# First attention of a fused attention and mixture kernel: where the sums of exponentials are formed, the order of the keys' products, the first weight decoding and the dummy products

## The chip, the cores and the metric

The kernel runs on one core of one Trainium2 chip. The metric is the device time of one execution in microseconds (us). Three executions before the change gave 999.26, 996.85 and 998.99, median 998.99. The core has five engines with a queue each, worked off in order: PE (matrix products; PEld is its loading of weights), DVE (vector), ACT (scalar functions), POOL (general), SP (here only issues DMA transfers). They wait for each other by semaphores.

## The reference

For 8 batches of 8 heads with 576 positions of 64 dimensions, a memory attention with 32 slots, then two layers of experts:

```python
a = np.exp(phi - np.max(phi, axis=2, keepdims=True))       # over the 576 positions
a = a / (np.sum(a, axis=2, keepdims=True) + 1e-09)
k_m = np.einsum('bhsm,bhsd->bhmd', a, k);  v_m = np.einsum('bhsm,bhsd->bhmd', a, v)
scores = (1 / np.sqrt(64)) * np.matmul(q, k_m.transpose(0, 1, 3, 2))
attn = softmax(scores);  out = np.matmul(attn, v_m)
# x: 4608 x 512
h = max(x @ w1, x @ w2, x @ w3);  y = h @ w_out             # weights arrive as float64
# second layer: of 8 experts the one with the largest gate, gate_w * relu(y @ w1[e]) @ w2[e]
```

## The kernel before, in words

Batches go one after another. The attention of batch b + 1 is woven into the first expert layer of batch b by a table of due times; the attention of batch 0 stands at the program's start, written out by hand (lines 843 to 893), and a scheduler turns that into one instruction order for each engine.

`phi` of a batch lies as 128 partitions by (4 pairs of heads j, 9 chunks c, 32 slots). A partition half `par` (64 partitions) belongs to one head of a pair. `at_max`, `at_col` and `at_sub` (lines 223 to 248) subtract the maximum, `at_exp` (L252) takes the exponential in two halves, pairs 0 and 1 first, then 2 and 3. `at_asum` (L254, through `over_chunks`, L218 to L221) adds the nine chunks elementwise: on DVE, for batch 1 on POOL. `at_km` (L260) multiplies: for each chunk, pair and half one product of 64 rows by 32 columns with 128 moving columns (64 of k, 64 of v), 72 products (L268), accumulated over chunks; each is two records in the trace, since its operands are float32. Then two products with a column of ones (L277) add the 64 partitions of `asum`. `rs` (L287, L288) is the reciprocal; with it ACT scales keys and values (`kx`, `vx`, L294 and L299). `at_kvT` transposes them on PE, ACT copies the result (`kT`, `vT`), DVE transposes q (`at_qT`, L319), PE forms the scores (L332), DVE transposes them back (L340), subtracts the maximum (L348), and so on to `at_hi` and `at_lo`, the first operand of the expert layer (`m1_step`, L101 to L103, with the maximum of the three branches on DVE, L458).

The float64 weights of the first layer come in 24 parts of 512 KB through six raw buffers. `w_done(n)` decodes one part to float32: ACT reads one word of each number (L151), DVE does four passes (L154, L161, L164, L167). A raw buffer is free after the last pass, and SP then issues the load of the part six further on. `after` (L125) is a copy of one element on ACT; it only makes what follows wait for its source.

`keep` (L840) issues products into a scratch bank that nobody reads. They hold TensorE busy. `WARM` (17 products, L758) is the same ahead of the first transpose.

Loads of batch 0 are issued by SP in the order of the code: phi, weights part 0, k, v, weights part 1, four of q, weights parts 2 to 5.

## Time and profile before

| | before |
|---|---|
| three executions | 999.26, 996.85, 998.99 us (median 998.99) |
| profiled execution | 1001.34 us, span of its instructions 999.6 us |
| PE busy | 970.2 us of the span (97%) |
| DVE busy | 563.5 us (56%) |
| ACT busy | 374.3 us (37%) |
| POOL busy | 150.8 us (15%) |
| granted TensorE clock, mean | 0.989 |

The busy time of PE counts the dummy products too, and it is an average over a start, a middle and an end with different limits. A time of a row is counted from the start of the span.

### The profile page before, as it was taken

The numbers are of one execution on the slowest core, as the hardware profiler recorded it, in microseconds if no ns is written. First come the engines' busy times: TensorE is split into PE (matmuls) and PEld (weight loads), VectorE is DVE, ScalarE is ACT, GpSimd is POOL, SyncE is SP. The second block draws the span as 40 slices with busy tenths as digits, with TensorE's granted clock in tenths as the row PEclk, the third lists the DMA queues.
The fourth block names the chain that finished last, engine by engine and source line by source line (L and its number), as shares of the span: only waits on it lengthen the run. The fifth ranks groups of instructions, "written<-read, shape, count | busy, mean of one in ns | idle before, by whom it ended". The sixth has DMA issues, their size and how long they took to land. (4 is left out here: it accounts for less than half of the span.)

```text
span 999.6 us, 20600 instructions
## 1 busy us (share of the span) xinstructions
PE 970.2 (97%) x8326; PEld 854.5 (85%) x8326; DVE 563.5 (56%) x1285; ACT 374.3 (37%) x816; POOL 150.8 (15%) x263
## 2 busy tenths in 40 slices
PE   7987999999999999999999999999999999999996
PEld 5566888889899888988889989898989898989985
DVE  5999768474674737747275626261717171726331
ACT  2574443433444334334356324150506060604220
POOL 0001021110211202122021030302021212111020
PEclk8998999999999999999999999999999999999998
DMA  9394342132221323010137426271717161625210
GB/s 330 114 338 152 120 125 92 48 121 96 101 80 38 129 86 121 13 37 2 48 104 244 134 58 207 44 220 35 229 32 231 33 206 52 204 57 159 96 34 26
DMA packets 59107, 114.79 MB, mean 115 GB/s; under 512 B 7687, under 2 KB 20999, under 8 KB 59008
## 3 DMA queue, kind: packets, MB, share of 16 engines
q1 hardware_dynamic: 48480, 94.01, 28.6%
q0 software_dynamic: 4768, 9.94, 4.3%
q10 hardware_dynamic: 5760, 9.48, 2.5%
q8 instruction: 67, 1.10, 0.5%
q14 instruction: 32, 0.26, 0.1%
HBM read 94.00 MB, written 19.44 MB: 113 GB/s over the span
## 5 line engine op out<-in xcount | busy, mean ns | idle before, releaser
L101 PE MATMUL ps_m<-at_hi,u_hi 128*128 128x288 f32 x576 | 175.4, 305 | 2.7 <-DVE hx L458 2.5
L103 PE MATMUL ps_m<-at_hi,u_lo 128*128 128x288 f32 x576 | 170.6, 297 | 0.2 <-ACT u_lo L435 0.2
L102 PE MATMUL ps_m<-at_lo,u_hi 128*128 128x288 f32 x576 | 169.9, 295 | 0.0
L101 PE MATMUL ps_x<-yh,w1h 128*128 128x288 f32 (+1 forms) x544 | 160.9, 296 | 0.3 <-DVE xh L625 0.3
L103 PE MATMUL ps_x<-yh,w1l 128*128 128x288 f32 (+1 forms) x544 | 159.9, 294 | 0.0
L102 PE MATMUL ps_x<-yl,w1h 128*128 128x288 f32 (+1 forms) x544 | 159.9, 294 | 0.0
L101 PEld LDWEIGHTS ps_m<-at_hi,u_hi 128*128 128x128 f32 x576 | 108.3, 188 | 25.2 <-issue 12.4
L458 DVE TENSOR_TENSOR hx<-hx,ps_m 128x288 f32<-128x288 f32 x192 | 86.1, 448 | 75.1 <-PE ps_m L103 67.5
L98 POOL TENSOR_TENSOR h_lo<-hx,h_hi 128x288 fp32r<-128x288 f32 x84 | 70.5, 839 | 380.9 <-ACT h_hi L97 359.6
L654 POOL DMA_DIRECT2D out_dram<-o x144 | 70.8, 498 | 352.6 <-DVE o L651 313.0
L101 PE MATMUL ps_m<-h_hi,wo_hi 128*128 128x288 f32 x384 | 115.0, 299 | 5.3 <-DVE hx L458 3.4
L102 PE MATMUL ps_m<-h_lo,wo_hi 128*128 128x288 f32 x384 | 113.7, 296 | 0.0
L103 PE MATMUL ps_m<-h_hi,wo_lo 128*128 128x288 f32 x384 | 113.6, 296 | 0.0
L103 PEld LDWEIGHTS ps_m<-at_hi,u_lo 128*128 128x128 f32 x576 | 108.0, 188 | 4.0 <-issue 3.1
L651 DVE TENSOR_SCALAR o<-ps_x,scal 128x512 f32<-128x512 f32 x32 | 24.0, 751 | 154.8 <-PE ps_x L103 154.8
L102 PEld LDWEIGHTS ps_m<-at_lo,u_hi 128*128 128x128 f32 x576 | 108.4, 188 | 0.9 <-issue 0.6
L101 PE MATMUL ps_x<-w2h,xh 128*128 128x512 f32 x272 | 107.6, 396 | 0.0
L102 PE MATMUL ps_x<-w2l,xh 128*128 128x512 f32 x272 | 107.5, 395 | 0.0
L103 PE MATMUL ps_x<-w2h,xh 128*128 128x512 f32 x272 | 107.4, 395 | 0.0
L101 PEld LDWEIGHTS ps_x<-yh,w1h 128*128 128x128 f32 x544 | 102.1, 188 | 1.8 <-ACT xh L622 0.5
L102 PEld LDWEIGHTS ps_x<-yl,w1h 128*128 128x128 f32 x544 | 102.1, 188 | 0.4
L103 PEld LDWEIGHTS ps_x<-yh,w1l 128*128 128x128 f32 x544 | 102.1, 188 | 0.0
(210 smaller groups left out, 1592.8 us busy)
## 6 DMA issues: line engine op xcount, KB each, us to landing
raw<-in_moe_w_dram SPq DMA_DIRECT2D x72, 512.0 KB, 4.8
raw<-y_dram SPq DMA_DIRECT2D x36, 288.0 KB, 3.1
w<-in_moe_w_dram SPq DMA_DIRECT2D x18, 512.0 KB, 5.2
kv_t<-in_k_dram SPq DMA_DIRECT2D x8, 1152.0 KB, 6.8
kv_t<-in_v_dram SPq DMA_DIRECT2D x8, 1152.0 KB, 9.7
q_t<-in_q_dram SPq DMA_DIRECT2D x32, 288.0 KB, 3.3
y_dram<-y_sb ACTq DMA_DIRECT2D x32, 288.0 KB, 2.1
out_dram<-o POOLq DMA_DIRECT2D x144, 64.0 KB, 1.9
```

Source lines behind the costliest of these rows:

```text
L98: eng.tensor_tensor(out=dst_lo, in0=src, in1=dst_hi, op=ALU.subtract)
L101: nc.tensor.matmul(out=ps, lhsT=hi_l, rhs=hi_r, start=first, stop=False)
L102: nc.tensor.matmul(out=ps, lhsT=hi_l, rhs=lo_r, start=False, stop=False)
L103: nc.tensor.matmul(out=ps, lhsT=lo_l, rhs=hi_r, start=False, stop=last)
L458: nc.vector.tensor_tensor(out=hx[0], in0=hx[0], in1=ps, op=ALU.max)
L651: nc.vector.tensor_scalar(out=o, in0=ps, scalar1=scal[:, b, t:t + 1], scalar2=None, op0=ALU.mult)
L654: nc.gpsimd.dma_start(out=out5[b, half, c], in_=o[i:i + TB])
```

## The change

In batches 0 and 1 the sums of exponentials are no longer added by DVE or POOL. PE forms them: for each chunk, pair and half one more product of the same exponentials with a column of ones, 72 products of one column, accumulated over the chunks. From batch 2 on nothing changes.

In batch 0 the keys' products run over pairs 0 and 1 for all chunks and then over pairs 2 and 3.

The decoding of weights part 0 starts behind `mb` instead of behind the exponential. The load of part 1 is issued behind the four of q. The decoding of part 1 stands behind the transposes of q. The transposes of q wait for `rs` instead of `kx`.

Dummies: 13 instead of 17 at the start; 8 and 8 with `mb` around the keys' products instead of 12 ahead; none between the products of the scores instead of 2; 1 instead of 2 behind part 2.

```diff
-    WARM = 17
+    WARM = 13
 ...
     def at_asum(b):
+        if b < 2:
+            return
 ...
-        over_chunks(asum, t, ALU.add, nc.gpsimd if b == 1 else nc.vector)
+        over_chunks(asum, t, ALU.add)
 ...
+        for js in ((0, 1), (2, 3)) if b == 0 else (range(J),):
+            for c in range(NCH):
+                for j in js:
 ...
+        if b < 2:
+            for c in range(NCH):
+                for j in range(J):
+                    for par in range(2):
+                        r0 = HP * par
+                        nc.tensor.matmul(
+                            out=pss[par][32 * j:32 * j + 32, 2 * D:2 * D + 1], lhsT=t[r0:r0 + HP, j, c, :], rhs=ones[r0:r0 + HP, 0:1],
+                            start=(c == 0), stop=(c == NCH - 1),
+                        )
 ...
-        w_load(1)
         for j in range(J):
             load_q(0, j)
-        for n in range(2, NRAW):
+        for n in range(1, NRAW):
             w_load(n)
 ...
+        w_done(0, mb[0:1, 0:1])
         at_sub(0)
-        keep(mb, 12)
+        keep(mb, 8)
         at_exp(0, 0)
-        w_done(0, inp["phi", 0][0:1, 0, 0, 0:1])
         at_exp(0, 1)
-        at_asum(0)
         at_km(0)
+        keep(mb, 8)
 ...
-        after(st["qT", 0][:, :, 0, 0, 0], kx[0:1, 0, 0, 0:J])
-        w_done(1, kx[0:1, 0, 0, 0:1])
+        after(st["qT", 0][:, :, 0, 0, 0], st["rs", 0][0:1].to_broadcast([1, J]))
         at_kvT(0)
-        turned = st["vT", 0][0:1, 0:1]
         for j in range(J):
             at_qT(0, j)
-        keep(st["qT", 0][:, 1].rearrange("p c e d -> p (c e d)")[:, :512], 2)
+        w_done(1, kx[0:1, 0, 0, 0:1])
+        turned = st["vT", 0][0:1, 0:1]
         at_scores(0)
         w_done(2, turned)
-        keep(wdst[2], 2)
+        keep(wdst[2], 1)
```

Behind line 250 a line number of the changed kernel is larger, by up to 16. PE's queue from the program's start, before (`warm` is the dummies' bank, `mb` the maxima spread out, `ps_kv` the keys' and values' bank, `w_97` the decoded weights):

```order
L758 MATMUL warm<-ones,ident 128x128 x17
L233 MATMUL ps_mx<-ident,mx 128x128
L244 MATMUL ps_mb<-ident,mb 128x128
L840 MATMUL warm<-mb,ident 128x128 x12
L268 MATMUL ps_kv<-kv_t,phi_t 32x128 x72
L277 MATMUL ps_kv<-ones,asum 128x1 x2
L305 MATMUL ps_kvT<-ident,kx 128x128 x2
L306 MATMUL ps_kvT<-ident,vx 128x128
L332 MATMUL ps_sc<-qT,kT 32x288
L840 MATMUL warm<-qT,ident 128x512 x2
L332 MATMUL ps_sc<-qT,kT 32x288 x31
L840 MATMUL warm<-w_97,ident 128x512 x2
```

The same place of PE's queue in the changed kernel:

```order
L774 MATMUL warm<-ones,ident 128x128 x13
L233 MATMUL ps_mx<-ident,mx 128x128
L244 MATMUL ps_mb<-ident,mb 128x128
L856 MATMUL warm<-mb,ident 128x128 x10
L272 MATMUL ps_kv<-kv_t,phi_t 32x128 x72
L285 MATMUL ps_kv<-ones,phi_t 32x1 x72
L856 MATMUL warm<-mb,ident 128x128 x6
L321 MATMUL ps_kvT<-ident,kx 128x128 x2
L322 MATMUL ps_kvT<-ident,vx 128x128
L348 MATMUL ps_sc<-qT,kT 32x288 x32
L856 MATMUL warm<-w_97,ident 128x512
```

Seventy-two one-column products stand between the keys' products and the transposes, and the second group of dummies is split, two of it ahead of the keys' products and six behind the sums. DVE's queue from the subtraction of the maximum to the transposes of q, before (`hc` and `asum` are the elementwise sums, `w_135` the raw part 0):

```order
L245 TENSOR_TENSOR phi_t<-phi_t,ps_mb 128x1152
L218 TENSOR_TENSOR hc<-phi_t 128x512
L219 TENSOR_TENSOR hc<-hc 128x4x64
L154 TENSOR_SCALAR w_97<-w_97 128x512
L220 TENSOR_TENSOR asum<-hc,phi_t 128x128
L161 TENSOR_SCALAR w_97<-w_97 128x512
L221 TENSOR_TENSOR asum<-asum,hc 128x128
L164 SCALAR_TENSOR_TENSOR w_97<-w_135,w_97 128x512
L167 SCALAR_TENSOR_TENSOR w_97<-w_135,w_97 128x512
L287 TENSOR_SCALAR rs<-ps_kv 128x1 x2
L288 RECIPROCAL rs<-rs 128x1 x2
L319 STREAM_TRANSPOSE qT<-q_t 128x576 x2
```

The same place of DVE's queue in the changed kernel, up to the first transpose of the scores (`w_131`, `w_144` are the raw parts 0 and 1):

```order
L245 TENSOR_TENSOR phi_t<-phi_t,ps_mb 128x1152
L154 TENSOR_SCALAR w_97<-w_97 128x512
L161 TENSOR_SCALAR w_97<-w_97 128x512
L164 SCALAR_TENSOR_TENSOR w_97<-w_131,w_97 128x512
L167 SCALAR_TENSOR_TENSOR w_97<-w_131,w_97 128x512
L302 TENSOR_SCALAR rs<-ps_kv 128x1 x2
L303 RECIPROCAL rs<-rs 128x1 x2
L335 STREAM_TRANSPOSE qT<-q_t 128x576 x4
L154 TENSOR_SCALAR w_97<-w_97 128x512 x2
L161 TENSOR_SCALAR w_97<-w_97 128x512 x2
L164 SCALAR_TENSOR_TENSOR w_97<-w_144,w_97 128x512
L356 STREAM_TRANSPOSE sc<-ps_sc 128x288
```

Four additions are gone, part 0 is decoded ahead of them all, and nothing stands between part 0 and `rs`, which waits for PE. On POOL four additions of batch 1 are gone; the rest of its queue is as before. From some 70 instructions on, the orders of DVE are the same, and PE's too but for the 72 sums of batch 1 where two products stood.

## Rows read from the trace of the kernel before

**Rows 1.** Busy time by stretch: us, PE, PEld, DVE, ACT, POOL busy (instructions), PEclk, DMA share, GB/s.

```profile
20.00:22.00 2.00, 2.00 (x3) 0.67 (x2) 2.00 (x4) 0.00 (x0) 0.00 (x0) 0.50 1.15 308
...
70.00:80.00 10.00, 7.03 (x80) 5.41 (x80) 9.86 (x18) 3.73 (x8) 3.53 (x4) 0.95 0.78 289
...
90.00:100.00 10.00, 6.64 (x36) 6.09 (x37) 10.00 (x25) 4.51 (x10) 0.00 (x0) 0.83 0.62 233
...
160.00:200.00 40.00, 40.00 (x349) 36.58 (x348) 22.68 (x52) 16.32 (x39) 5.85 (x7) 1.00 0.19 60
```

**Rows 2.** Timeline of PE, 75 to 110: start, us, instruction, idle before and releaser.

```profile
77.98 0.40 PE L101 MATMUL ps_m<-at_hi,u_hi 128*128 128x288 f32 x1 [1.70 <-DVE hx L458]
...
88.61 0.39 PE L277 MATMUL ps_kv<-ones,asum 64*128 64x1 f32 x4
88.93 0.40 PE L101 MATMUL ps_m<-at_hi,u_hi 128*128 128x288 f32 x1
...
93.53 0.40 PE L101 MATMUL ps_m<-h_hi,wo_hi 128*128 128x288 f32 x1 [2.59 <-DVE hx L458]
...
109.82 0.40 PE L101 MATMUL ps_m<-h_hi,wo_hi 128*128 128x288 f32 x1 [1.90 <-ACT y_sb L475]
```

**Rows 3.** Timeline of DVE, 70 to 85, the decoding passes beside POOL's additions.

```profile
70.87 0.42 DVE L154 TENSOR_SCALAR w<-w 128x512 f32<-128x512 f32 x1
...
74.31 1.52 DVE L154 TENSOR_SCALAR w<-w 128x512 f32<-128x512 f32 x1
75.75 1.21 DVE L167 SCALAR_TENSOR_TENSOR w<-w,w 128x512 uint32<-128x512 uint32 x1
76.89 0.67 DVE L161 TENSOR_SCALAR w<-w 128x512 uint32<-128x512 uint32 x1
...
78.82 0.68 DVE L167 SCALAR_TENSOR_TENSOR w<-w,w 128x512 uint32<-128x512 uint32 x1
...
83.09 0.42 DVE L161 TENSOR_SCALAR wod<-wod 128x512 uint32<-128x512 uint32 x1
84.67 0.69 DVE L98 TENSOR_TENSOR wo_lo<-wod,wo_hi 128x512 fp32r<-128x512 f32 x1 [1.16 <-ACT wo_hi L97]
```

**Rows 4.** Timeline of POOL, 60 to 130: first and last of four additions.

```profile
74.10 1.44 POOL L218 TENSOR_TENSOR hc<-phi_t 128x512 f32<-128x512 f32 x1 [72.78 <-ACT phi_t L252]
...
77.35 0.52 POOL L221 TENSOR_TENSOR asum<-asum,hc 128x128 f32<-128x128 f32 x1
```

**Rows 5.** Timeline of all engines, 0 to 45.

```profile
1.38 6.88 PE L758 MATMUL warm<-ones,ident 128*128 128x128 f32 x34 [1.38 <-POOL ident masks.py:199]
...
9.26 2.84 PE L840 MATMUL warm<-mb,ident 128*128 128x128 f32 x24
...
10.85 1.26 ACT L252 ACTIVATE phi_t<-phi_t 128x576 f32<-128x576 f32 x2 [1.81 <-DVE phi_t L245]
...
12.04 2.31 PE L268 MATMUL ps_kv<-kv_t,phi_t 64*32 64x128 f32 x144
...
15.61 0.22 DVE L287 TENSOR_SCALAR rs<-ps_kv 128x1 f32<-128x1 f32 x2
...
16.94 0.44 PE L305 MATMUL ps_kvT<-ident,kx 128*128 128x128 f32 x2 [2.13 <-ACT kx L294]
...
17.19 1.44 DVE L319 STREAM_TRANSPOSE qT<-q_t 128x576 f32<-128x576 f32 x2 [1.16 <-ACT qT L125]
...
23.07 0.28 PEld L332 LDWEIGHTS ps_sc<-qT,kT 32*32 32x32 f32 x32 [1.50 <-issue]
...
25.03 1.21 DVE L340 STREAM_TRANSPOSE sc<-ps_sc 128x288 f32<-128x288 f32 x3 [1.84 <-PE ps_sc L332]
...
28.41 1.42 DVE L348 TENSOR_TENSOR sc<-sc,smx 128x576 f32<-128x576 f32 x2
...
39.91 0.69 PE L101 MATMUL ps_m<-at_hi,u_hi 128*128 128x288 f32 x1
```

**Rows 6.** DMA issues 2.3 to 2.8: transfer, count, KB, us from issue to landing.

```profile
kv_t<-in_v_dram SPq DMA_DIRECT2D x1, 1152.0 KB, 9.5
```

## The prediction

> **What bounds the kernel now.** I read the busy times by stretch first, then the waits of PE from 75 to 110, then what DVE and POOL do there, and last the start, instruction by instruction. By stretch the reader is to see two regimes. From 160 on PE has no idle time (40.00 of 40) while DVE has (22.68): PE is the bound. From 70 to 100 it is the other way round: DVE is busy for 9.86 and 10.00 of 10 us while PE has 7.03 and 6.64 [rows 1]. In that part DVE still decodes the float64 weights. PE's waits say the same: 1.70 at 77.98 and 2.59 at 93.53 both end with DVE's maximum (L458), and the last one, 1.90 at 109.82, ends with an ACT copy that stands behind the second attention's exponentials, which follow DVE too [rows 2]. After it PE runs on. So a microsecond of DVE time saved ahead of 104 is a microsecond at the end, and a microsecond of PE time added ahead of 93 is free as long as it fits into 1.70 and 2.59.

> The start is a chain: maximum, exponential (10.85 to 12.11), keys' products (12.04), sums, `rs` on DVE (15.61), scaling on ACT, transposes of q (17.19), scores, and DVE's subtraction of the maximum, which ends at 28.41 + 1.42 = 29.83 [rows 5]. [...]

> **The change part by part.** Times are against the profiled execution: span 999.6, 1001.34 with what lies around it, 2.35 above the median of 998.99.

> POOL's additions of batch 1 go. They run from 74.10 to 77.87 [rows 4]. DVE's passes beside them are long: L154 takes 1.52 against 0.42 earlier, L167 1.21 against 0.68 later, L161 0.67 against 0.42 [rows 3]. The excess is 1.10 + 0.53 + 0.25 = 1.88. DVE is the bound there, so the term is -1.9. No other row has a reason for it: the passes' operands are the same as in the short ones. PE's wait of 1.70 at 77.98 goes with it. Of DVE's wait of 1.16 at 84.67 (for an ACT copy that stands behind a chain over PE) [rows 3] a part goes when PE is earlier by that; I take half, -0.5, with the ends 0 and -1.16.

> PE's 72 sums in batch 1 replace two products, four records, that hold PE from 88.61 to 88.93, 0.32 [rows 2]. The trace has no one-column products on 64 by 32. The nearest rows: the keys' products have the same 144 weight loads of the same weights, and 144 records take 2.31 with the last one's own 0.27, so 2.04. From below, 32 loads on 32 by 32 take 0.28, 0.0088 each, so 144 take 1.26 [rows 5]. From above, the four records in 0.32 use two tiles of the array, 0.08 each; spread over four times as many tiles that is 0.02, 2.9 for 144. I take 2.04, the same loads. In batch 1 that adds 1.7 to PE, behind which PE waits 2.59 for DVE: 0 on the path. If that cover went, it would cost 1.7.

> The start. Four dummy products fewer (eight records of 34 in 6.88) let the first transpose start about 1 us earlier, since the maximum is done before [rows 5]. The subtraction and the exponential come 1 us earlier. It gains nothing: the keys' products need v, which is issued at 2.3 and lands 9.5 later, at 11.8 [rows 6]. Before they start at 12.04 anyway. Splitting by pairs so that the first half can start behind the first exponential therefore buys nothing either; by then both are done.

> The split has a price. The dummies with `mb`, 24 records of 128 columns in 2.84, show 0.112 for a record of 128 columns once the last one's tail of 0.16 is off [rows 5]. One after another, 144 such records would take 16.1. The keys' products take 2.04, so eight run side by side: the eight combinations of pair and half, each with its own 64 rows and 32 columns of the array. With two pairs at a time there are four, and two tiles' own records can't run at once: 16.1 / 4 = 4.0. Ends: 2.04, if the array hides it all the same, and 4.0. I take 4.0.

> So PE ends the keys' products at 11.85 + 4.0 = 15.85, the sums at 17.9, and DVE starts `rs` at about 18.1 instead of 15.61: 2.5 late. DVE has nothing in its queue between part 0 (now decoded by 12, beside the wait for v and PE) and `rs`, so it idles for 6. Behind `rs` DVE's work is the same before and after: 29.83 - 15.61 less the waits of 1.16 and 1.84 [rows 5], 11.2, since parts 1 and 2 are decoded there in both. One wait stays, for the scaling on ACT ahead of q's transposes (1.2). The wait for the scores goes: the four transposes now run without passes between them, and then five passes, 2 us, cover the scores' products. 18.1 + 1.2 + 11.2 = 30.5 against 29.83: +0.7 for the start. With the ends above (2.04 + 1.26 and 4.0 + 2.9) `rs` is at 15.4 or 19.0, and the start -2.0 or +1.6.

> In other words, the additions taken from DVE and its waits, some 4.6 with 1.32 for the exponential, are given back as a wait for PE.

> [...] The keys' records start 0.014 apart on average (2.04 / 144) [rows 5]. [...]

> Moves that cost nothing: part 0's copy on ACT (0.7) stands ahead of the exponential, beside DVE's subtraction; q's loads are 512 KB earlier on SP's queue, part 1's load four transfers later, and part 1 is decoded 4 us after it can land. The load of part 6 is issued earlier, as part 0 is free earlier; DMA is busy then anyway. Should part 1 land late, its pass would hold the scores' transposes behind it. The first expert product (39.91) stands behind dummies [rows 5]; of these one product of 512 columns, about 0.9, is gone, which meets the +0.7. DVE, not PE, then sets the pace.

> Sum: +0.7 - 1.9 - 0.5 = -1.7. Span 997.9, and 998.99 - 1.7 = 997.3 for the median.

> **The rivals.**
> 1. The pairs cost nothing and the sums are short: `rs` at 15.4 to 16.1, the start -2.0, total -4.4: 994.6. For it: the records need not fill the array to be fast, and no row has four tiles of this form. Against: 16.1 / 2.04 = 7.9 fits eight tiles too well.
> [...]
> 3. The sums take 2.9, the upper end: `rs` 0.9 later, batch 1 another 0.9 still within PE's wait: 998.2. For it: 0.08 a record is the only row with one column. Against: those records have 128 columns of weights to load, these 32. [...]
> 4. DVE's gain in 74 to 78 is hidden: the next bound behind it, the loads of weights and the chains over ACT and PE that make the waits of 1.16 and others near 103, holds DVE where it was: 998.99 + 0.7 = 999.7. For it: DMA is at 0.78 of its time in that stretch [rows 1]. Against: raw buffers come free when DVE is done with them, so loads move with DVE.

> **How the numbers follow.** Forecast 0.40, rivals 0.24, 0.11, 0.12, 0.13. What a measurement can tell from no change is 0.3%, 3.0 us: below 996.0 is faster, above 1002.0 slower. The forecast's own range is 995.7 to 998.8, from the half wait of 84.67 and the sums' bounds. Faster: most of rival 1 (0.20) and a quarter of the forecast, 0.30. Slower: half of rival 2 and a little of the rest, 0.09. Range 993.8 to 1001.0: it takes in rival 1's centre and rivals 3 and 4, and leaves out half of 2.

> **What would show it.** In the changed profile: no POOL instruction ahead of the first expert split of batch 1, L154, L161 and L167 at 0.42 and 0.68 all through 70 to 80, PE's wait at 78 gone. The keys' products of batch 0 start at 11.8 to 12.0 and end near 15.9; the 144 one-column records end near 17.9; `rs` near 18.1; DVE idle for 6 ahead of it; the last subtraction of the maximum near 30.5. PE's restart, 109.82 before, at about 108.1. The prediction is wrong where the keys' products take 2, where the clock is at 0.50 from 12 to 18, or where the restart does not move with DVE.

## The result and the profile after

| | before | after |
|---|---|---|
| median of 14 executions each, us | 999.09 (994.62 to 1003.00) | 1003.17 (1000.74 to 1007.20) |
| ratio to before | | 1.0053 [1.0039, 1.0067] |
| profiled execution, us | 1001.34, span 999.6 | 1001.74, span 1000.0 |
| PE's restart behind the last wait for `y_sb` | 109.82 [rows 2] | 112.64 |

The change makes the kernel slower by about 4 to 5 us, where 1.7 less were forecast. The two profiled executions differ by only 0.4, since that of before is 2.3 above its median and that of after 1.4 below. So the first 113 us are compared row by row. Behind the restart PE runs on but for short stops, and the rest of a profiled execution, its time less its restart, was 887.8 to 891.5 in all kernels here.

The timeline of PE in the changed kernel, 6 to 36: start, us, instruction, in brackets the idle time before and what ended it.

```profile
12.03 3.42 PE L272 MATMUL ps_kv<-kv_t,phi_t 64*32 64x128 f32 x132 [1.74 <-DMA kv_t<-in_v_dram]
...
15.56 0.46 PE L285 MATMUL ps_kv<-ones,phi_t 64*32 64x1 f32 x21
18.67 1.22 PE L285 MATMUL ps_kv<-ones,phi_t 64*32 64x1 f32 x114 [2.64 <-issue]
19.81 2.93 PE L856 MATMUL warm<-mb,ident 128*128 128x128 f32 x12
22.54 0.63 PE L321 MATMUL ps_kvT<-ident,kx 128*128 128x128 f32 x2
24.05 0.48 PE L322 MATMUL ps_kvT<-ident,vx 128*128 128x128 f32 x1 [0.88 <-issue]
25.00 2.73 PE L348 MATMUL ps_sc<-qT,kT 32*32 32x288 f32 x64 [0.47 <-ACT kT L325]
31.85 2.04 PE L856 MATMUL warm<-w,ident 128*128 128x512 f32 x2 [4.12 <-DVE w L167]
```

These answer to rows 5. In the middle of the sums, after 30 of 144 records, PE stands still for 2.64, and again for 0.88 ahead of the last transpose. Nothing that the profile shows ended either ("issue"): the sums that follow the first stop read exponentials that were read a moment before. On DVE (timeline, 15 to 35) `rs` comes at 19.91 instead of 15.61, and the last subtraction ends at 33.83 instead of 29.83.

```profile
19.91 0.22 DVE L302 TENSOR_SCALAR rs<-ps_kv 128x1 f32<-128x1 f32 x2 [8.21 <-PE ps_kv L285]
...
21.48 2.76 DVE L335 STREAM_TRANSPOSE qT<-q_t 128x576 f32<-128x576 f32 x4 [1.16 <-ACT qT L125]
...
33.07 0.76 DVE L364 TENSOR_TENSOR sc<-sc,smx 128x576 f32<-128x576 f32 x1
```

By stretch (us, then busy time of PE, PEld, DVE, ACT, POOL with instructions, granted clock, DMA share, GB/s), the rows that answer to rows 1:

```profile
20.00:25.00 5.00, 3.65 (x16) 2.96 (x16) 3.39 (x9) 2.29 (x9) 0.00 (x0) 0.50 0.77 221
25.00:30.00 5.00, 2.72 (x64) 1.33 (x64) 3.92 (x10) 0.99 (x3) 0.00 (x0) 0.50 0.03 9
30.00:35.00 5.00, 3.15 (x18) 0.72 (x18) 4.93 (x9) 1.37 (x2) 0.00 (x0) 0.50 0.62 206
70.00:80.00 10.00, 7.18 (x58) 5.22 (x57) 9.70 (x22) 6.42 (x14) 0.00 (x0) 1.00 1.01 383
90.00:100.00 10.00, 8.04 (x258) 7.94 (x240) 10.00 (x21) 4.95 (x9) 0.00 (x0) 0.69 0.68 236
```

The granted clock is 0.50 from 18.7, as the stop ends, to 35.8. DVE, which is to be the bound, is idle for 1.61 and 1.08 of 5 us from 20 to 30: it waits for the scores. In 70 to 80 POOL is gone. There DVE's passes have their short times (timeline of DVE, 74 to 90), and `wo_lo`, which waited 1.16 [rows 3], waits for nothing:

```profile
80.15 0.42 DVE L154 TENSOR_SCALAR w<-w 128x512 f32<-128x512 f32 x1
80.49 0.68 DVE L167 SCALAR_TENSOR_TENSOR w<-w,w 128x512 uint32<-128x512 uint32 x1
81.09 0.42 DVE L161 TENSOR_SCALAR w<-w 128x512 uint32<-128x512 uint32 x1
...
87.37 0.68 DVE L98 TENSOR_TENSOR wo_lo<-wod,wo_hi 128x512 fp32r<-128x512 f32 x1
```

In batch 1 PE stops among the sums too (timeline of PE, 81 to 115), hidden in what was a wait of 2.59 [rows 2]:

```profile
91.08 0.99 PE L285 MATMUL ps_kv<-ones,phi_t 64*32 64x1 f32 x87
94.03 0.69 PE L285 MATMUL ps_kv<-ones,phi_t 64*32 64x1 f32 x53 [1.96 <-issue]
...
112.64 0.40 PE L101 MATMUL ps_m<-h_hi,wo_hi 128*128 128x288 f32 x1 [1.90 <-ACT y_sb L491]
```

The lag of an instruction is how much later it starts than the same instruction before. Followed through the trace: first expert product 44.15 against 39.91 [rows 5], +4.24; +5.86 at DVE's column maximum (L235; 76.16 against 70.30); +3.95 at the maximum of the three branches once POOL's stretch is passed (81.43 against 77.48), so -1.91; +2.70 at `wo_lo`, -1.25; +2.82 at the restart. Of the rise by 1.6 between 45 and 76 the groups of PE's instructions by line (36 to 74: busy, mean ns, idle before) show a wait of 1.9 for ACT's copy `hx`; before, the same group waits 0.6 for DVE and not for ACT.

```profile
L101 PE MATMUL ps_m<-at_hi,u_hi 128*128 128x288 f32 x46 | 14.4, 313 | 2.3 <-ACT hx L472 1.9 <-DVE hx L474 0.4
```

These lags belong to two executions, and that of after is the third fastest of its 14. They explain 2.8 of a loss of 4.1 between the medians; where the other executions lose the rest was not recorded.

### The profile page after: what moved, and what is told of

Same layout as the page of the kernel before. It is cut to its first block, busy times and chain, and to the rows that moved or that the text cites. A ratio compares the mean times of both kernels' runs of the same rounds, so it can differ in the third digit from the quotient of the medians.

```text
span 1000.0 us, 21133 instructions
## 1 busy us (share of the span) xinstructions
PE 968.0 (97%) x8600; PEld 858.1 (86%) x8600; DVE 559.2 (56%) x1281; ACT 374.5 (37%) x816; POOL 146.9 (15%) x259
## 3 DMA queue, kind: packets, MB, share of 16 engines
q8 instruction: 69, 1.13, 0.5%
## 5 line engine op out<-in xcount | busy, mean ns | idle before, releaser
L101 PEld LDWEIGHTS ps_m<-at_hi,u_hi 128*128 128x128 f32 x576 | 108.6, 189 | 26.7 <-issue 11.8
```

The source lines that it names most:

```text
L101: nc.tensor.matmul(out=ps, lhsT=hi_l, rhs=hi_r, start=first, stop=False)
```

## The experiments

What could make PE stop: A, it has used up its instructions and the next ones have not come; or the products by pairs, one-column products as such, or the dummies and the clock. For A the trace has one lead. The profile's DMA queue 8, "instruction", moved a packet of 16384 bytes from 16.13 to 17.18 and one from 21.57 to 22.72, and each stop ended 1.3 to 1.5 after one of them. The transfers of 16 to 17, by queue (packets, MB, share of 16 engines):

```profile
q1 hardware_dynamic: 349, 0.35, 103.3%
q8 instruction: 1, 0.02, 6.6%
```

Every kernel ran in five rounds beside the kernel before (three for the quiet transfers).

**All pairs at once.** The order of the keys' products of batch 0 is put back:

```diff
-        for js in ((0, 1), (2, 3)) if b == 0 else (range(J),):
+        for js in (range(J),):
```

> The changed kernel with the keys' products of batch 0 over all four pairs again. Theory A (instruction supply: PE works off the small products faster than its instructions are brought in, and stops once for about 2.7 us in the sums): the keys' products take 2.0 to 2.2 instead of 3.5 and the stop stays, 2 to 3 us; rs comes 0.5 to 1.5 earlier than 19.9, and the time is 0.5 to 2 below the changed kernel's. Rival B (the stop belongs to one-column products, say their writes into one bank): the same stop, at the same record of the sums. Rival C (the pairs cost nothing): rs at 19.9 and the same time.

1002.74, ratio 1.0055 [1.0034, 1.0076], as the change. The timeline of PE has the stops in the same places:

```profile
16.09 0.64 PE L285 MATMUL ps_kv<-ones,phi_t 64*32 64x1 f32 x20
19.12 1.18 PE L285 MATMUL ps_kv<-ones,phi_t 64*32 64x1 f32 x116 [2.39 <-issue]
...
25.87 0.33 PE L322 MATMUL ps_kvT<-ident,vx 128*128 128x128 f32 x1 [2.71 <-issue]
```

So the pairs aren't the cause. `rs` came at 20.32, not 0.5 to 1.5 earlier than 19.91 as A had it. The comparison of the two orders is spoilt: here the clock was at 0.50 from 13.2 to 16.6.

**Batch 0's sums on DVE again.** All else as in the change (`if b < 2` becomes `if b == 1` in `at_asum` and `at_km`, with `at_asum(0)` ahead of `at_km(0)`).

> The changed kernel with the sums of batch 0 formed on DVE again, and on PE in batch 1 only. Theory A and rival B alike: no stop at the start, rs near 16.0 (keys' products by pairs from 12.0 to 15.5, then four records), 3.9 earlier; the time is 4 to 5.5 below the changed kernel's, 997.5 to 999. Rival D (the loss is the low clock through other dummies, not the sums): the clock is at 0.50 from 18 to 35 all the same and the time is within 1.5 of the changed kernel's.

997.51, ratio 0.9996 [0.9979, 1.0012], 5.7 below the change; no stop, `rs` at 16.18, PE's restart at 105.75. Pairs, dummies, decoding and loads are all in this kernel, so they don't carry the loss. Set against the next kernel, which has none of them (995.41), they cost 2.1 together; the two intervals overlap. Its keys' products show the price of the pairs, 3.75 with the last record's tail against 2.31 [rows 5], at the pace of the change, where the clock was 1.00 (132 in 3.42):

```profile
12.09 3.75 PE L272 MATMUL ps_kv<-kv_t,phi_t 64*32 64x128 f32 x144 [1.75 <-DMA kv_t<-in_v_dram]
15.77 0.39 PE L292 MATMUL ps_kv<-ones,asum 64*128 64x1 f32 x4
```

**Only batch 1's sums on PE**, in the kernel before:

```diff
     def at_asum(b):
+        if b == 1:
+            return
...
-        over_chunks(asum, t, ALU.add, nc.gpsimd if b == 1 else nc.vector)
+        over_chunks(asum, t, ALU.add)
```

and the 72 one-column products in `at_km` for `b == 1`.

> The kernel before with nothing changed but the sums of batch 1, on PE instead of POOL. The prediction's terms: DVE's passes beside POOL go back from 1.52, 1.21 and 0.67 to 0.42, 0.68 and 0.42, 1.9 less, and the wait of 1.16 for wo_hi goes, so about 3 below the kernel before: 996. A stop of 2 us in the sums of batch 1 lies in PE's wait for DVE. Rival: the stop there is not covered, or DVE is held by the loads of weights, and the time is within 1 of the kernel before.

995.41 against 998.01, ratio 0.9972 [0.9954, 0.9990]; restart at 105.42. This part of the change is a gain, of the size forecast (-1.9 and -0.5 to -1.2). In its trace the lag is -1.14 at DVE's column maximum (69.16 against 70.30) and -4.28 at `wo_lo` (80.39 against 84.67), so -3.14 between them.

**Dummies between keys' products and sums**, 12 of them, in the changed kernel:

> The changed kernel with 12 more dummy products of 128 columns between the keys' products and the sums of batch 0 (10 of them land there, 2.2 us at full clock). Theory A: they give the supply of instructions time; the stop in the sums shrinks by about as much as they take, and rs comes within 0.6 of 19.9. Rival B (a stop of the one-column products themselves): the stop stays at 2.7 and rs comes 2 later, at 22. The time follows rs, within 1 of the changed kernel by A, 2 more by B.

1006.26, ratio 1.0074 [1.0051, 1.0096]. Timeline of PE:

```profile
16.15 2.50 PE L284 MATMUL warm<-mb,ident 128*128 128x128 f32 x20
18.58 0.25 PE L289 MATMUL ps_kv<-ones,phi_t 64*32 64x1 f32 x10
19.13 1.24 PE L289 MATMUL ps_kv<-ones,phi_t 64*32 64x1 f32 x128 [0.30 <-issue]
25.33 0.28 PE L289 MATMUL ps_kv<-ones,phi_t 64*32 64x1 f32 x6 [4.96 <-issue]
```

Later stops of this kind stand at 193 plus a multiple of 256 too, and the kernel before has them as well. There they are short, and its runs of small products are half as long, 288 instructions: 0.46 ahead of record 4033 in the keys' products of a later batch (timeline of PE, 204 to 206), and 0.56 ahead of record 6849 at 327.50.

```profile
204.85 0.62 PE L268 MATMUL ps_kv<-kv_t,phi_t 64*32 64x128 f32 x18 [0.46 <-issue]
```

In the timelines shown here the stops last 0.30 to 4.96.

**The same sums with a quarter of the instructions.** The exponentials lie chunk first, so one product adds all four pairs, 18 products a batch for 72:

```diff
+                    nc.tensor.matmul(
+                        out=pss[par][:, 2 * D:2 * D + 1], lhsT=st["cm", b][r0:r0 + HP, c].rearrange("p j m -> p (j m)"),
+                        rhs=ones[r0:r0 + HP, 0:1], start=(c == 0), stop=(c == NCH - 1),
+                    )
```

> The changed kernel, but the exponentials of batches 0 and 1 lie chunk first, so that one product of 128 columns of exponentials by the column of ones adds all four pairs: 18 products a batch instead of 72, a quarter of the instructions for the same sums. Theory A: PE's instructions come in blocks of 256, and a block is only there some 5.4 us after PE has entered the block ahead of it (in the changed kernel the stops stand ahead of records 449 and 705 of PE, 256 apart, and so they do with all pairs at once and with dummies between, whatever the products there). Record 449 now falls 12 records ahead of the end of the sums: a stop there that ends at 18.7 (18.3 to 19.4), rs at 18.9 instead of 19.91, time about 1000.5 (998.5 to 1002.5). Rival B: the stop comes from a burst of too many small products; with 72 records instead of 288 there is none, rs at 16.3 as with the sums on DVE, time 997.5 (996 to 999).

and the same with 32 instructions fewer ahead of the sums (`WARM` 9, `keep(mb, 6)`), and no `keep` behind `at_km`, so six dummies fewer behind them:

> As the run with merged sums, with 8 dummy products (32 instructions) fewer ahead of the sums: 9 at the start and 6 and none around the keys' products, instead of 13, 8 and 8. Theory A: record 449 now falls behind the sums and the transposes of keys and values, among the scores: no stop in the sums, rs at 16.3 (16.0 to 16.9), a short stop or none among the scores at about 18.5 to 19, time 997.5 (996 to 999.5), 3 below the run with merged sums. Rival B: no stop in either, the two within 1 us of each other. If the clock falls for want of dummies, up to 2 us more, which its records would show ahead of 20 us.

1000.32 (1.0023 [1.0005, 1.0040]) and 998.05 (0.9995 [0.9979, 1.0012]). PE's timeline of the first, and then of the second:

```profile
15.79 1.94 PE L288 MATMUL ps_kv<-ones,cm 64*128 64x1 f32 x30
18.68 0.49 PE L288 MATMUL ps_kv<-ones,cm 64*128 64x1 f32 x6 [0.95 <-issue]
```

```profile
12.02 5.38 PE L276 MATMUL ps_kv<-kv_t,cm 64*32 64x128 f32 x144 [2.63 <-DMA kv_t<-in_v_dram]
17.33 2.17 PE L288 MATMUL ps_kv<-ones,cm 64*128 64x1 f32 x36
```

In the first the stop stands ahead of record 449 again, now six records before the end of 36, and ends at 18.68 as foretold (`rs` at 19.10); in the second record 449 is among the scores, at 22.73, and the sums have no stop. Fewer products alone (rival B) would have spared the first its stop. Two things were missed in the second: `rs` came at 19.54 instead of 16.3, because the clock was at 0.50 from 12.6 to 16.0, and because these records have 0.056 each, 2.0 for 36, no less than 144 of the small ones.

So the time of the second, forecast at 997.5, came out right by luck: its `rs` is later than the first's, and so is its restart (110.38 against 109.66). Its lead of 2.3 arises behind the restart. There the first stops ahead of records 2753, 5569 and 8385, for 2.2 in all, the second once, for 0.88; the rest of the lead is not explained. The longest of these stops (timeline of PE in the first, 138 to 145):

```profile
143.03 0.51 PE L276 MATMUL ps_kv<-kv_t,phi_t 64*32 64x128 f32 x17 [1.34 <-issue]
```

What the pair shows is where the stop falls, not what it costs.

**No loads beside the sums.** In the changed kernel parts 1 to 6 of the weights wait for `rs`:

```diff
-        for n in range(1, NRAW):
-            w_load(n)
...
+        for n in range(1, NRAW + 1):
+            w_load(n, st["rs", 0][0:1, 0:1])
```

> The changed kernel, but the loads of weight parts 1 to 6 wait for rs, so that no load runs beside the sums of batch 0 (weights come later, so its time says little). Theory A with the loads as cause of the late blocks: record 193 is entered at 13.2 and the next block is there about 3.3 us later, as in batch 1 (3.0 to 3.6 us there), not 5.45: the stop ahead of record 449 shrinks from 2.64 to below 0.9, rs at 17.7 (17.0 to 18.4). Rival C: a block takes its 5.4 us at the start whatever else is loaded (first touch, distance to memory): stop 2.6, rs at 19.9. Time 999 to 1006 by either.

PE's timeline, and the transfers of 14 to 15 by queue:

```profile
15.94 0.46 PE L285 MATMUL ps_kv<-ones,phi_t 64*32 64x1 f32 x21
16.84 1.12 PE L285 MATMUL ps_kv<-ones,phi_t 64*32 64x1 f32 x114 [0.44 <-issue]
```

```profile
q1 hardware_dynamic: 603, 0.15, 64.9%
q8 instruction: 1, 0.02, 5.5%
```

The stop is 0.44, `rs` at 18.01. Record 193 is entered at 13.60, the packet starts at 14.41, where the loads run out, and the next block is usable at 16.83: 3.23, as in batch 1, not 5.4. The fixed delay (rival C) falls. Though its weights come later, this kernel takes 999.18, ratio 1.0022 [1.0003, 1.0041] where the change has 1.0053.

From entering a block to the next one being usable, where PE stopped for it (in batch 1 of the other kernels with its sums in small products it was 2.9 to 3.7):

| | entered | usable | us |
|---|---|---|---|
| change | 13.22 | 18.67 | 5.45 |
| change, next block | 18.67 | 24.05 | 5.38 |
| all pairs | 13.26; 19.12 | 19.12; 25.86 | 5.86; 6.74 |
| dummies between | 13.67; 19.13 | 19.13; 25.33 | 5.46; 6.20 |
| sums merged | 13.31 | 18.68 | 5.37 |
| batch 0's sums only (below) | 12.71; 18.60 | 18.60; 24.80 | 5.89; 6.20 |
| quiet transfers | 13.60; 16.83 | 16.83; 20.29 | 3.23; 3.46 |
| change, batch 1 | 90.47 | 94.03 | 3.56 |

**Only batch 0's sums on PE**, in the kernel before:

> The kernel before with only batch 0's sums as one-column products (batch 1's stay on POOL; order of the keys' products, decoding, loads and dummies as before): the disputed edit by itself. Theory A (PE's instructions come in blocks of 256, here under loads 5.4 to 6.7 us after PE entered the block ahead): PE enters record 193 at 12.5 to 13; the keys' products begin at record 125 and end at 412, so the stop falls 36 records into the sums and ends at about 18 to 19.5; the sums end at 19.3 to 20.8, ahead of record 705, which falls into the transposes of keys and values and stops PE again; rs at 19.5 to 21 against 15.61 before. Time 1002.5 (1000 to 1005), about 4.5 above the kernel before. Rival B (pairs, dummies, loads or decoding have the loss): 998 to 999.5.

1003.83 against 997.91, ratio 1.0068 [1.0047, 1.0089]. Timeline of PE:

```profile
14.26 0.32 PE L282 MATMUL ps_kv<-ones,phi_t 64*32 64x1 f32 x17
18.60 1.29 PE L282 MATMUL ps_kv<-ones,phi_t 64*32 64x1 f32 x126 [4.02 <-issue]
21.25 0.69 PE L317 MATMUL ps_kvT<-ident,kx 128*128 128x128 f32 x2 [1.36 <-ACT kx L306]
24.80 0.48 PE L318 MATMUL ps_kvT<-ident,vx 128*128 128x128 f32 x1 [2.86 <-issue]
```

Stops ahead of records 449 and 705, `rs` at 19.91, restart at 117.98. The disputed edit alone costs as much as the whole change (+0.68% against +0.53%, with intervals that overlap).

**Three versions meant to be fast**, all from the kernel before with batch 1's sums on PE. Part 1 decoded in DVE's wait for the keys' products:

> A version meant to be fast: the kernel before with batch 1's sums as one-column products (995.4 in its run), the decoding of weights part 0 behind mb, and that of part 1 behind the sums of exponentials, so that 2.2 us of DVE's work lie in its wait for the keys' products. Theory A has nothing against it (sums of batch 0 stay on DVE, so PE's block that starts at record 449 is not wanted before 19 us): rs at 16.2, part 1 decoded by then, the last subtraction of the maximum about 1.5 us earlier than in the run it is built on, time 994.2 (993 to 996). If the wait for the keys' products is too short for it, rs at 17 and 995.4 to 996.5.

997.40, ratio 1.0002 [0.9985, 1.0020]. The scheduler put part 1's passes ahead of `rs`, at 16.85 against 15.20, and the clock fell to 0.50 from 18.2 to 25.0. Fewer dummies (`keep(wdst[2], 1)`, `keep(wdst[0], 8)`):

> A version meant to be fast: the kernel before with batch 1's sums as one-column products, with 1 dummy instead of 2 behind weights part 2 and 8 instead of 10 behind part 0. In the run it is built on, the four products of the first two dummies hold the u products until 28.3, ACT waits with u_lo, and DVE stands idle from 32.2 to 33.95 for the decoding behind ACT; the last dummies end 2.1 us after the second at_lo. If DVE's wait there is on the path: first m1 product at 37.3 instead of 38.67, time 994.3 (993.3 to 995.4), ratio 0.9963 to the kernel before. If DVE is held by ACT for another reason, or the clock falls for want of dummies: 995 to 996.5.

998.57, ratio 1.0006 [0.9985, 1.0028]. The first expert product came at 36.86, even earlier than foretold, but batch 1's column maximum at 72.56 instead of 69.16. Without the dummies the scheduler laid ACT and DVE out anew: PE's group in 36 to 74 now waits 3.5 for ACT's `hx`, for which the version it is built on had no wait.

```profile
L101 PE MATMUL ps_m<-at_hi,u_hi 128*128 128x288 f32 x52 | 15.9, 317 | 3.9 <-ACT hx L468 3.5 <-DVE hx L470 0.4
```

And with part 0 decoded early as well:

> As the version with fewer late dummies, with the decoding of weights part 0 behind mb as in the changed kernel: DVE no longer has 1.4 us of it between the sums and rs, so rs comes at 14.7 instead of 15.2 and everything behind it 0.5 earlier: 993.9 (992.8 to 995.2). If the keys' products set rs, no difference between the two (within 0.7).

998.00, ratio 0.9995 [0.9977, 1.0014], within 0.7 of the one before, `rs` at 15.13 for 15.27. None beats the version with batch 1's sums alone. That one stays the best measured, 0.9972.

## Why the prediction was wrong

- The step that failed: "the sums at 17.9, and DVE starts `rs` at about 18.1". The sums were priced by how close records can follow each other, 2.04 for 144, and the wait for PE's own instructions has no term. At that pace PE needs a new block of 256 instructions in less time than one takes to come: keys' products and sums are 576 instructions, forecast in 6 us, so 256 in 2.7, where a block took 5.4. The records themselves cost even less than forecast: 30 in 0.8 and 114 in 1.2. `rs` came 1.8 late, and the stop between the records, 2.64, is the whole of that and more: 19.91 less the stop is 17.3, an estimate. Shown by the kernels with that edit alone, without it, with fewer instructions, and with quiet transfers.
- What was built on it: 12.4 from `rs` to the last subtraction became 13.9. The dummies behind the sums ran at a granted clock of 0.50 (2.93 for 12 records, where they take 1.60 with the sums on DVE), the second stop held the transposes, and DVE waited for scores. The gap of 0.7 that was to be met by a dummy less became 4.24 at the first expert product.
- Right: the keys' products' start at 12.03 on v, and their price by pairs (forecast 4.0, measured 3.5, or 3.75 with the last record's tail); DVE idle ahead of `rs`.
- Right, and so not rival 4: POOL's term, -1.88 forecast, -1.91 measured by lags. The wait of 1.16 went wholly, where half was taken.
- Right, though not for the price given: batch 1's sums lie within PE's wait. They have a stop of 1.96 of their own, which fits in as well: from `wo_lo` to the restart the lag grows by 0.12.
- Missed, and read from one trace only: 1.6 between 45 and 76, with PE waiting for ACT's `hx`. The new order of ACT is a likely cause, since fewer dummies made the same wait; it wasn't tried by itself in the changed kernel.
- None of the three signs of being wrong that the prediction names came up: the keys' products took 3.5, the clock was 1.00 from 12 to 18, and the restart moved with DVE. The sign was `rs` at 19.91 where 18.1 was forecast.
- Rival 2, which the chances and the range count with, had a clock that falls ahead of the keys' products. The trace of the changed kernel does not show that: the clock was 1.00 from 12 to 18 and 0.50 only from 18.7, as the first stop ended. Rival 3's sums did end late, but not because a record is slow: 114 on 64 by 32 took 1.22 with the last one's tail, some 10 ns each.

In sum: batch 0's sums alone +0.68% [0.47, 0.89], batch 1's alone -0.28% [-0.46, -0.10], together +0.40; the change +0.53% [0.39, 0.67]. The rest, +0.13, is within the uncertainty.

## What to carry to other kernels

Count instructions, not only time: where many small products stand in a row, ask how long 256 of PE's instructions last, and whether the next 256 can come meanwhile (in these runs 2.9 to 3.7 us in batch 1 and with quiet transfers, 5.4 to 6.7 beside loads). Where PE was idle by "issue" in the middle of such a run here, at record numbers 256 apart, it went on 1.3 to 1.6 after a packet of the queue "instruction" had landed; that was the sign that it waited for its program. Split a change that helps in one place and hurts in another: batch 1's half of this one was worth having alone.

## What the runs showed of the hardware that was not expected

- Beside data a load of instructions came later. In the rows of the table its packet started 2.8 to 4.2 after PE had entered the block while the DMA engines were full (share 1.05 to 1.13). With quiet transfers and in batch 1 it started 0.8 to 1.1 after. It took 0.9 to 1.3, and PE went on 1.3 to 1.6 after it had landed.
- Taking out 32 instructions ahead of the sums moved record 449, and the stop with it, out of them: it stood six records before their end, with a stop to 18.68, and then among the scores, at 22.73. So dummy products counted in the blocks too, with four instructions for one of float32 (in the change 26 weight loads and 26 products for the 13 at the start).
- Products on different tiles of the array ran side by side: 144 keys' records of 128 moving columns took 2.31 on eight tiles [rows 5] and 3.75 on four (batch 0's sums on DVE), where the 24 dummies of 128 columns on the whole array took 2.84 [rows 5]. And 36 records with 128 columns of weights and one moving column took 2.0 (merged, 32 fewer), no less than 144 of the small ones.
